# Attention outputs of three batches as plain float32 products, and decay arithmetic moved between VectorE, GpSimd and ScalarE

## The chip, the cores and the metric

The kernel runs on one core of a Trainium2 chip. The metric is the device time of one launch in microseconds (us). The engines are named as the profile names them: PE (TensorE's matmuls; PEld is its weight loads), DVE (VectorE), ACT (ScalarE), POOL (GpSimd) and SP (SyncE, which only issues DMAs here). Each engine takes its instructions in a fixed order, so whatever stands behind a waiting instruction waits too.

## The reference

Cut down, three parts that follow each other, for 4 batches of 768 tokens and 384 columns (8 heads of 48):

```python
def _attn_ref(q, k, v, a_re, a_im):
    mag = np.sqrt(a_re * a_re + a_im * a_im)
    scale = np.minimum(mag, 0.999) / (mag + 1e-06)
    a_re_n, a_im_n = (a_re * scale, a_im * scale)
    for t in range(S):
        new_re = ar * S_re - ai * S_im
        new_im = ar * S_im + ai * S_re
        S_re, S_im = (new_re + kv, new_im)
        y[:, :, t] = np.einsum('bhd,bhde->bhe', q[:, :, t], S_re)
def _moe_ref(x, U, V, w_ch1, w_ch2):
    u = x + (xt @ U @ V).transpose(0, 2, 1)
    return u + np.maximum(u @ w_ch1, 0.0) @ w_ch2
def _moe2_ref(x, w_ch1, w_ch2):
    u = x + np.real(fft2(x))
    return u + np.maximum(norm(u) @ w_ch1, 0.0) @ w_ch2
```

Here kv is the outer product of a token's key and value, xt is x transposed, and fft2 runs over tokens and columns. The first part is a linear attention with a complex decay for every token, head and channel; the other two are two-layer blocks with 1536 hidden columns.

## The kernel before, in words

The attention runs in chunks of 128 tokens, two chunks ("a pair") at a time: 6 chunks and 3 pairs to a batch, `m` counting the 12 pairs. Four generators of Python code build it.

- `decays(m)` works on tiles of 128 partitions by 768 columns (3 channel groups x 2 chunks x 128 tokens). L326 to L360 normalise the decays, take running products along the tokens (the scan of L340, one for each of 3 channel groups), and scale the queries (L359) and keys (L360). In batches 1 to 3 POOL does L325, L337, L349, L354 and L360, and L359 too in two pairs.
- `turns(m)` takes running sums of the angles (the scan of L381, three to a pair) and their sine and cosine, and L408 and L409 multiply queries and keys by these into the tile `QK`; POOL does one of the four products of each chunk. Six DMAs then move each chunk's `QK` into the transposed tile `QT`.
- `products(m, j)` works on one chunk: scores `sc` (L437), masked scores `pm` (L442), transposed keys `kp` (L451), outputs `y` and the contribution to the state `g` (both L469, in `summed`). Batch 0 and the first 4 chunks of batch 1 are `plain`: `y` and `g` are float32 products, head by head, of column halves of the array (0 to 63 and 64 up). From chunk 4 of batch 1 on, every factor is first split into two float16 parts (`ph`, `vh` and `vl`, `qh` and `ql`, `kh` and `kl`, `Sh` and `Sl`; POOL makes the low part of `ph` at L446 and of `Sl` at L568, ACT and DVE the others), and three float16 products, 128 columns wide, stand for one float32 product.
- `moe_units(0, ...)` is the first two-layer block. For each hidden step it multiplies into `hp` (9 matmuls, L91 to L93), ACT makes `hh` (L182) and DVE makes its low part `hl` (L184) with high priority, and one step later 9 matmuls add the step's output to `acc`.

`first_attention` runs batch 0's attention by itself. Then batch b's two-layer block runs with the attention of batch b + 1 spread between its steps (`Side`); batch 3's runs with the transform of batch 0 beside it; last come the second two-layer blocks. The order on every engine is fixed ahead by a scheduler that runs its own timing model over the priorities of this code (`schedule_with_timeline_sim`). Tiles named `t` come from a ring of 6 buffers, and a pair of batches 1 to 3 uses four of them (T, L, s, Th); slots tagged `x1` come from a ring of 3.

Of the kernel before, what the change touches and what calls it, by code (L numbers as in the profile page):

```python
# [8 lines left out]
F16 = mybir.dt.float16  # L9
# [12 lines left out]
DM = H * D  # L22
# [7 lines left out]
GSCALE = 2.0**-10  # L30
YSCALE = 2.0**-10 / FSCALE
# [10 lines left out]
def mixer_kernel(ctx, tc, a_in, qk_in, v_in, u_in, v4_in, w_in, cc_in, ss_in, cb_in, sb_in, id_in, mask_in, rows_in, out):  # L42
# [148 lines left out]
    # ------------------------------------------------------------------ attention  # L191
# [27 lines left out]
    def load(kind, m):  # L219
        """Decays, or queries and keys, of a pair of chunks."""  # L220
# [4 lines left out]
        if b == 0:  # L225
            t = wpl.tile(shape, F32, tag="w", name=name)
        else:
            t = attention_pool()(name, f"{kind}in", 1, shape)
# [3 lines left out]
    def load_vs():  # L232
        """All values of the first batch."""
# [15 lines left out]

    def row(x, i, js):  # L250
        return x[:, i, js].rearrange("p j t -> p (j t)")

    def parts(m):
        """The first pair goes chunk by chunk, so that its products start early."""
        return [slice(0, 1), slice(1, 2)] if m == 0 else [slice(0, 2)]

    def decays(m):
        """Decayed queries and keys of a pair of chunks and the tangents of its turns."""
# [3 lines left out]
        E = G if b else V  # L262

# [13 lines left out]
        ew[m] = T_, Th, qf, kf, ends  # L277
# [87 lines left out]
    def turns(m):  # L365
        """Rotates the queries and keys of a pair of chunks."""
        b, cc = PAIRS[m]
        at = attention_pool()
        T_, Th, qf, kf, ends = ew[m]
# [6 lines left out]
        for js in jj:  # L376
            cy = carry.get(b)
            t, th = T_[:, :, js], Th[:, :, js]
            n = 128 * (js.stop - js.start)
            for i in range(3):  # L380
                V.tensor_tensor_scan(  # L381
                    out=row(Th, i, js),
                    data0=one.to_broadcast([128, n]),
                    data1=row(T_, i, js),
                    initial=0.0 if cy is None else cy[:, i : i + 1],
                    op0=ALU.mult,
                    op1=ALU.add,
                )
# [12 lines left out]
            for j in range(js.start, js.stop):  # L401
# [14 lines left out]
    def products(m, j):  # L416
        """Scores, outputs and the next state of one chunk."""
# [4 lines left out]
        plain = b == 0 or b == 1 and c < 4  # L422
# [17 lines left out]
        def masked(hf):  # L440
            pm.append(room[:, hf] if b == 0 else at(f"pm{n}_{hf}", "pm", 2, (128, 4, 128)))
# [21 lines left out]
        def summed(out, rows, ops):  # L463
# [20 lines left out]
        if not plain:  # L484
# [3 lines left out]
            ph, plo = t3("ph", 1, (128, 2, 8, 128), F16).rearrange("p s h t -> s p h t")  # L488
# [9 lines left out]
        if not plain and c > 0:  # L498
# [726 lines left out]
```

## Time and profile before

| | |
|---|---|
| device time, 3 runs | 1037.37, 1039.2 and 1039.5 us; median 1039.2 |
| span of the profiled execution | 1035.1 us |
| what lies around the span | 2.3 to 4.4 us, by the three runs' times |
| busy, whole span | PE 885.1, DVE 690.3, POOL 443.3, ACT 441.3 us |
| 128 to 530 us (attention of batches 1 to 3 beside the first block) | PE 332.6, DVE 325.1, POOL 225.8, ACT 229.4 of 402 us; clock 0.90 |

The profiled execution has no time of its own beside its span; it is set against the three runs by what lies around it. A PE that is busy is not a PE at its peak, since matmuls overlap and their ends are modelled; PEclk is the granted clock as a share of the full 2.4 GHz.

### The profile page before, as it was taken

What the parts mean: (1) busy time and instruction counts of PE and PEld (TensorE: products, weight loads), DVE (VectorE), ACT (ScalarE), POOL (GpSimd) and SP (SyncE); (2) the same over time, 40 slices, a digit from 0 to 9 for tenths busy, and PEclk for the clock granted to TensorE, in tenths of its full rate; (3) what the DMA queues carried; (4) which work ended last, traced back from release to release, by engine and by line L of the source; (5) the groups of instructions that cost most, each with busy time, mean ns of one, the idle gap of its engine ahead of it and who ended that gap; (6) DMA issues with size and microseconds to landing.
All of it is one profiled execution on the core that took longest, in us unless ns stands there. A gap on an engine that the chain in (4) does not pass through costs nothing. (4 is left out here: it accounts for less than half of the span.)

```text
span 1035.1 us, 16471 instructions
## 1 busy us (share of the span) xinstructions
PE 885.1 (86%) x6338; PEld 841.7 (81%) x6338; DVE 690.3 (67%) x1104; ACT 441.3 (43%) x841; POOL 443.3 (43%) x426
## 2 busy tenths in 40 slices
PE   0059978788778787798899999779999999999997
PEld 0048777578777787787899999779999999999997
DVE  7997988897877689788764727886535554362121
ACT  6436565657545555555643224465212211222111
POOL 4445646575464645656446307776312222020000
PEclk9999899979898898989899999889999999999999
DMA  8078646834516152614135103342101021000000
GB/s 346 0 103 165 194 81 138 166 69 109 94 45 121 49 93 69 115 48 93 33 61 200 39 1 115 108 144 77 62 16 47 2 77 46 1 23 19 7 23 27
DMA packets 47097, 83.43 MB, mean 81 GB/s; under 512 B 5600, under 2 KB 36064, under 8 KB 47008
## 3 DMA queue, kind: packets, MB, share of 16 engines
q1 hardware_dynamic: 45152, 75.96, 30.8%
q0 software_dynamic: 1856, 6.31, 1.7%
q8 instruction: 52, 0.85, 0.4%
q14 instruction: 37, 0.30, 0.1%
HBM read 53.79 MB, written 9.44 MB: 61 GB/s over the span
## 5 line engine op out<-in xcount | busy, mean ns | idle before, releaser
L184 DVE SCALAR_TENSOR_TENSOR hl<-hp,hh 128x384 fp32r<-128x384 f32 x192 | 105.4, 551 | 191.8 <-ACT hh L182 186.6
L182 ACT ACTIVATE hh<-hp 128x384 fp32r<-128x384 f32 x192 | 93.1, 488 | 270.9 <-PE hp L93 249.1
L91 PE MATMUL acc<-w,hh 128*128 128x384 f32 x576 | 202.4, 352 | 2.0 <-ACT hh L182 2.0
L93 PE MATMUL acc<-w,hl 128*128 128x384 f32 x576 | 166.1, 352 | 38.4 <-DVE hl L184 38.2
L92 PE MATMUL acc<-w,hh 128*128 128x384 f32 x576 | 197.4, 343 | 0.0
L93 PEld LDWEIGHTS acc<-w,hl 128*128 128x128 f32 x576 | 106.9, 195 | 45.4 <-DVE hl L184 45.1
L91 PEld LDWEIGHTS acc<-w,hh 128*128 128x128 f32 x576 | 111.4, 193 | 4.3 <-ACT hh L182 3.0
L92 PEld LDWEIGHTS acc<-w,hh 128*128 128x128 f32 x576 | 111.5, 194 | 0.0
L91 PE MATMUL hp<-u,w 128*128 128x384 f32 x288 | 103.0, 359 | 6.2 <-ACT w L141 3.1
L92 PE MATMUL hp<-u,w 128*128 128x384 f32 x288 | 103.7, 360 | 1.2 <-POOL u L630 1.0
L93 PE MATMUL hp<-u,w 128*128 128x384 f32 x288 | 102.4, 356 | 0.0
L92 PE MATMUL hp<-n,w 128*128 128x384 f32 x288 | 96.9, 336 | 1.6 <-DVE n L920 1.6
L91 PE MATMUL hp<-n,w 128*128 128x384 f32 x288 | 96.5, 336 | 1.1 <-ACT n L919 1.1
L93 PE MATMUL hp<-n,w 128*128 128x384 f32 x288 | 96.8, 336 | 0.0
L437 PE MATMUL sc<-QT 96*128 96x128 f32 x384 | 66.6, 328 | 11.4 <-DMA QT<-QK 10.5
L437 PEld LDWEIGHTS sc<-QT 96*128 96x128 f32 x384 | 60.7, 232 | 14.3 <-issue 11.3
L142 POOL TENSOR_TENSOR w<-wxw,w 128x384 fp32r<-128x384 f32 x48 | 58.8, 1235 | 21.9 <-ACT w L141 21.7
L451 PE MATMUL kp<-ident,QK 128*128 128x128 f32 x120 | 20.5, 297 | 53.7 <-POOL QK L409 48.6
L91 PEld LDWEIGHTS hp<-u,w 128*128 128x128 f32 x288 | 58.5, 203 | 7.0 <-ACT w L141 3.3
L451 PEld LDWEIGHTS kp<-ident,QK 128*128 128x128 f32 x120 | 16.1, 155 | 55.5 <-POOL QK L409 48.6
L92 PEld LDWEIGHTS hp<-u,w 128*128 128x128 f32 x288 | 58.6, 203 | 2.2 <-POOL u L630 1.6
L93 PEld LDWEIGHTS hp<-u,w 128*128 128x128 f32 x288 | 58.3, 203 | 0.0
(302 smaller groups left out, 2056.4 us busy)
## 6 DMA issues: line engine op xcount, KB each, us to landing
QT<-QK SPq DMA_DIRECT2D x144, 129.0 KB
stw<-in_w_dram SPq DMA_DIRECT2D x48, 384.0 KB
ain<-in_a_dram SPq DMA_DIRECT2D x12, 768.0 KB
qkin<-in_qk_dram SPq DMA_DIRECT2D x12, 768.0 KB
x1d<-x SPq DMA_DIRECT2D x24, 192.0 KB
vin<-in_v_dram SPq DMA_DIRECT2D x18, 192.0 KB
lo<-x1d SPq DMA_DIRECT2D x12, 192.0 KB
out_dram<-lo SPq DMA_DIRECT2D x12, 192.0 KB
```

The lines of the kernel that those rows point to most:

```text
L91: T.matmul(o, ah, bh, start=start, stop=False, skip_group_check=skip)
L92: T.matmul(o, ah, bl, start=False, stop=False, skip_group_check=skip)
L93: T.matmul(o, al, bh, start=False, stop=stop, skip_group_check=skip)
L142: G.tensor_tensor(w[:, 1, zs], x, f32(w[:, 0, zs]), ALU.subtract)
L182: A.activation(hh, hp, AF.Relu)
L184: V.scalar_tensor_tensor(out=hl, in0=hp, scalar=0.0, in1=f32(hh), op0=ALU.max, op1=ALU.subtract)
L437: T.matmul(ps[:, h, :], q[:, 128:256], q[:, :128], start=True, stop=True)
L451: T.transpose(kp[z][:, i * 128 : (i + 1) * 128], QK[:, z, i, 128:256], ident)
```

## The change

Outputs `y` of batches 1 to 3 become float32 products of column halves in all chunks, as batch 0 has them; with them go `ph`, `qh`, `ql`, `Sh` and `Sl`. The state's `g`, on the other hand, becomes float16 products in the first 4 chunks of batch 1 as well. On the decays, L325 goes from POOL to ACT in batches 1 to 3 (9 pairs); L349 and L354 go from POOL to DVE there, L359 in 2 pairs; one scan takes the place of three, over 768 columns, with restarts from the constant tiles `starts` and `going`. The four products into `QK` become two, twice as wide, both on DVE. The angles are worked out in place in the tile of decays, of which there are now two by turns, so T and Th need no buffers; the count of L291 writes to an `x1` slot instead. The rest of the diff drops comments and moves constants.

```diff
+        s1, s2 = mk("L"), mk("s")
+        qf, kf = (qk[:, 0], qk[:, 1]) if b == 0 else (s1, s2)
+        Th, T_ = a[:, 0], a[:, 1]
...
-            E.tensor_scalar(s2_, s2_, -2e-6, 1.0, ALU.mult, ALU.add)
+            if b:
+                A.activation(s2_, s2_, AF.Identity, bias=one, scale=-2e-6)
+            else:
+                V.tensor_scalar(s2_, s2_, -2e-6, 1.0, ALU.mult, ALU.add)
...
-            n = 128 * (js.stop - js.start)
-            for i in range(3):
-                V.tensor_tensor_scan(out=row(s1, i, js), data0=starts[:, :n], data1=row(s1, i, js), initial=1.0, op0=ALU.max, op1=ALU.mult)
-        if b:
+            V.tensor_tensor_scan(out=flat(s1), data0=starts, data1=flat(s1), initial=1.0, op0=ALU.max, op1=ALU.mult)
+        if b and attp[1]:
             load("a", m + 1)
...
-            (G if m == 2 or b else V).tensor_tensor(th, s1_, th, ALU.mult)
+            (G if m == 2 else V).tensor_tensor(th, s1_, th, ALU.mult)
...
-            (G if m in (1, 2) or b else V).tensor_tensor(s1_, s1_, s2_, ALU.mult)
+            (G if m in (1, 2) else V).tensor_tensor(s1_, s1_, s2_, ALU.mult)
...
-            (G if m in (1, 2, 3, 4) else V).tensor_tensor(f, q, s1_, ALU.mult)
+            (G if m in (1, 2) else V).tensor_tensor(f, q, s1_, ALU.mult)
...
+            if len(jj) == 1:
+                if cy is not None:
+                    V.tensor_tensor(T_[:, :, 0, 0], T_[:, :, 0, 0], cy[:, :3], ALU.add)
+                V.tensor_tensor_scan(out=flat(Th), data0=going, data1=flat(T_), initial=0.0, op0=ALU.mult, op1=ALU.add)
+            else:
+                for i in range(3):
+                    V.tensor_tensor_scan(
...
-                for z, w in ((1, T_), (0, Th)):
-                    V.tensor_tensor(QK[:, z, :, :128], qf[:, :, j], w[:, :, j], ALU.mult)
-                    (V if z else G).tensor_tensor(QK[:, z, :, 128:256], kf[:, :, j], w[:, :, j], ALU.mult)
+                w = a[:, :, :, j]
+                V.tensor_tensor(QK[:, :, :, 128:256], kf[:, :, j].unsqueeze(1).to_broadcast([128, 2, 3, 128]), w, ALU.mult)
+                V.tensor_tensor(QK[:, :, :, :128], qf[:, :, j].unsqueeze(1).to_broadcast([128, 2, 3, 128]), w, ALU.mult)
+                for z in range(2):
...
-        plain = b == 0 or b == 1 and c < 4
+        plain = b == 0
...
+            pm.append(room[:, hf] if b == 0 else at(f"pm{n}_{hf}", "pm", 2, (128, 4, 128), pl=attp[1]))
             V.tensor_tensor(pm[hf], sc[hf], mask.unsqueeze(1).to_broadcast([128, 4, 128]), ALU.mult)
-            if not plain:
-                hs = slice(hf * 4, hf * 4 + 4)
-                A.copy(ph[:, hs], pm[hf])
-                G.tensor_tensor(plo[:, hs], pm[hf], ph[:, hs], ALU.subtract)
...
-                    for p in (slice(0, 64), slice(64, rows)) if plain else (slice(0, 128),):
+                    for p in (slice(0, 128),) if whole else (slice(0, 64), slice(64, rows)):
...
+        if not plain and not last:
             vh, vl = t3("vh", 2, (128, DM), F16), t3("vl", 2, (128, DM), F16)
             A.activation(vh, vin, AF.Copy, scale=VSCALE)
             V.scalar_tensor_tensor(out=vl, in0=vin, scalar=VSCALE, in1=vh, op0=ALU.mult, op1=ALU.subtract)
-            ph, plo = t3("ph", 1, (128, 2, 8, 128), F16).rearrange("p s h t -> s p h t")
...
-        if not plain and c > 0:
-            qh, ql = t3("qh", 1, (96, 8, 128), F16), t3("ql", 1, (96, 8, 128), F16)
-            A.copy(qh, QT[:, :, :128])
-            V.tensor_tensor(ql, QT[:, :, :128], qh, ALU.subtract)
...
-        if not plain and c > 0 and not isinstance(S, tuple):
-            S = t3("S", 2, (96, DM)), t3("Sh", 1, (96, DM), F16), t3("Sl", 1, (96, DM), F16)
-            A.activation(S[0], state[b], AF.Copy, scale=GSCALE * KSCALE * VSCALE)
-            A.copy(S[1], S[0])
-            G.tensor_tensor(S[2], S[0], S[1], ALU.subtract)
...
-        if plain:
-            ops = [(lambda h: pm[h // 4][:, h % 4], vin)]
-            if S is not None:
-                ops.append((lambda h: QT[:, h, :128], S))
-        else:
-            ops = [(lambda h: ph[:, h], vh), (lambda h: ph[:, h], vl), (lambda h: plo[:, h], vh)]
-            if S is not None:
-                pS, shi, slo = S
-                ops += [(lambda h: qh[:, h], shi), (lambda h: qh[:, h], slo), (lambda h: ql[:, h], shi)]
+        ops = [(lambda h: pm[h // 4][:, h % 4], vin)]
+        if S is not None:
+            ops.append((lambda h: QT[:, h, :128], S))
...
-                summed(gp, 128, [(hs(kh), vh), (hs(kh), vl), (hs(kl), vh)])
+                    G.tensor_tensor(sh, S.rearrange("p (h e) -> p h e", h=8), f3, ALU.mult)
+                summed(gp, 128, [(hs(kh), vh), (hs(kh), vl), (hs(kl), vh)], whole=True)
...
-            shi, slo = t3("Sh", 1, (96, DM), F16), t3("Sl", 1, (96, DM), F16)
-            A.copy(shi, sS)
-            G.tensor_tensor(slo, sS, shi, ALU.subtract)
-            state[b] = sS, shi, slo
+            state[b] = sS
```

The scheduler then orders every engine anew. Three places show what that does. On PE, in batch 2, chunk 1 (y_1 the output, g_1 the contribution to the state; the first number of a name is the chunk, the last only a buffer). Before:

```order
L469 LDWEIGHTS kh_1_2899
L469 MATMUL g_1_3015<-vh_1_2840,kh_1_2899 128x48
L469 LDWEIGHTS qh_1_2872
L469 MATMUL y_1_2947<-Sh_0_2809,qh_1_2872 128x48
L469 LDWEIGHTS kh_1_2899
L469 MATMUL g_1_3015<-vh_1_2840,kh_1_2899 128x48
L469 LDWEIGHTS qh_1_2872
L469 MATMUL y_1_2947<-Sh_0_2809,qh_1_2872 128x48
```

And now, at the same place on PE:

```order
L469 MATMUL y_1_2874<-vin_1_2669,pm_1_1_2828 64x48 x8
L469 MATMUL y_1_2874<-S_0_2718,QT_1_2298 64x48 x3
L469 LDWEIGHTS kh_1_2830
L469 MATMUL g_1_2926<-vh_1_2781,kh_1_2830 128x48
L469 MATMUL y_1_2874<-S_0_2718,QT_1_2298 64x48
L469 LDWEIGHTS kh_1_2830
L469 MATMUL g_1_2926<-vh_1_2781,kh_1_2830 128x48
L469 MATMUL y_1_2874<-S_0_2718,QT_1_2298 64x48
```

The two kinds of product alternate one by one in both, but now a column half of `y` stands between two full-width products of `g`; 94 halves of `y` in batches 2 and 3 stand so.

On DVE, in batch 2, the stretch around `hl` of hidden step 5 of the block of batch 1 (hl_1_0_5: batch, group, step; L, s and QK are the pair's tiles). Before:

```order
L184 SCALAR_TENSOR_TENSOR hl_1_0_4_2924<-hp_1_0_4_2885,hh_1_0_4_2922 128x384
L326 SCALAR_TENSOR_TENSOR L_4_3111<-L_4_3111,s_4_3112 128x768
L340 SCALAR_TENSOR_TENSOR L_4_3111<-starts,L_4_3111 128x256 x3
L461 SCALAR_TENSOR_TENSOR kl_2_3148<-kp_2_0_3151,kh_2_3147 128x8x48
L184 SCALAR_TENSOR_TENSOR hl_1_0_5_3046<-hp_1_0_5_3005,hh_1_0_5_3044 128x384
```

Now, on DVE:

```order
L412 TENSOR_TENSOR QK_3_2863<-L_2_2589,ain_2_2124 128x6x128
L183 SCALAR_TENSOR_TENSOR hl_1_0_4_2853<-hp_1_0_4_2818,hh_1_0_4_2851 128x384
L326 SCALAR_TENSOR_TENSOR L_4_3016<-L_4_3016,s_4_3017 128x768
L338 SCALAR_TENSOR_TENSOR L_4_3016<-starts,L_4_3016 128x768
L183 SCALAR_TENSOR_TENSOR hl_1_0_5_2957<-hp_1_0_5_2916,hh_1_0_5_2955 128x384
```

The normalisation and the running product still stand ahead of `hl`, the latter as one instruction.

On POOL, the instructions of the same pair around L325 and L337 (ph the float16 scores, T the tangents). Before:

```order
L568 TENSOR_TENSOR Sl_1_3050<-S_1_3016,Sh_1_3049 96x384
L325 TENSOR_SCALAR s_4_3112<-s_4_3112 128x768
L446 TENSOR_TENSOR ph_2_3105<-pm_2_0_3129,ph_2_3105 128x512
L337 TENSOR_TENSOR T_4_3110<-ain_4_2704,Th_4_3113 128x768
L446 TENSOR_TENSOR ph_2_3105<-pm_2_1_3143,ph_2_3105 128x512
```

Now, on POOL:

```order
L493 TENSOR_TENSOR QK_2_2840<-QK_2_2840 128x3x128
L337 TENSOR_TENSOR ain_4_2657<-ain_4_2657 128x768
L490 TENSOR_SCALAR fe_2_3012<-QT_2_2842 96x8
L493 TENSOR_TENSOR QK_2_2840<-QK_2_2840 128x3x128
```

Of the run of five, L337 is left, between two products with the chunk's end decays (L494 before, L493 now).

## Rows read from the trace of the kernel before

**Rows 1.** Busy time by stage, core 0; the header names the columns.
```profile
core 0: us, PE busy (x) PEld busy (x) DVE busy (x) ACT busy (x) POOL busy (x), PEclk, DMA share, GB/s
128.00:530.00 402.00, 332.61 (x2650) 310.37 (x2651) 325.08 (x428) 229.35 (x415) 225.79 (x195) 0.90 0.42 86
```

**Rows 2.** Waits of PE, 128 to 530 us: total us, times, longest us.
```profile
PE acc L93 <- DVE hl L184: 31.4, 12, 6.4
PE g L469 <- DVE kl L461: 15.1, 6, 5.4
```

**Rows 3.** Timeline of DVE: start us, length us, instruction, count, idle before.
```profile
341.99 4.79 DVE L326 SCALAR_TENSOR_TENSOR L<-L,s 128x768 f32<-128x768 f32 x1 [2.78 <-POOL s L325]
346.82 1.86 DVE L340 TENSOR_TENSOR_SCAN L<-starts,L 128x256 f32<-128x256 bf16 x3
```

**Rows 4.** Timeline of POOL, beside rows 3.
```profile
341.12 0.84 POOL L325 TENSOR_SCALAR s<-s 128x768 f32<-128x768 f32 x1
341.92 1.17 POOL L446 TENSOR_TENSOR ph<-pm,ph 128x512 f16<-128x512 f32 x1
343.05 1.81 POOL L337 TENSOR_TENSOR T<-ain,Th 128x768 f32<-128x768 f32 x1
344.82 1.15 POOL L446 TENSOR_TENSOR ph<-pm,ph 128x512 f16<-128x512 f32 x1
```

**Rows 5.** Timeline of PE around one stall.
```profile
160.42 0.91 PE L93 MATMUL acc<-w,hl 128*128 128x384 f32 x3 [2.63 <-DVE hl L184]
161.13 0.53 PE L91 MATMUL hp<-u,w 128*128 128x384 f32 x1
161.45 0.53 PE L92 MATMUL hp<-u,w 128*128 128x384 f32 x1
```

**Rows 6.** DVE's groups by shape, whole span: count, busy us, mean ns, idle before.
```profile
L340 DVE TENSOR_TENSOR_SCAN L<-starts,L 128x256 f32<-128x256 bf16 x36 | 37.6, 1097 | 0.1
L381 DVE TENSOR_TENSOR_SCAN Th<-one,cy,T 128x256 f32<-128x256 f32 x18 | 29.5, 1683 | 0.0
L326 DVE SCALAR_TENSOR_TENSOR L<-L,s 128x768 f32<-128x768 f32 x12 | 26.3, 2189 | 17.0 <-POOL s L325 16.8
L501 DVE TENSOR_TENSOR ql<-QT,qh 96x1024 f16<-96x1024 f32 x12 | 16.9, 1406 | 2.8 <-ACT qh L500 2.7
L354 DVE TENSOR_TENSOR L<-L,s 128x768 f32<-128x768 f32 x1 | 1.0, 959 | 0.0
```

**Rows 7.** Timeline of DVE: two scans while POOL rests.
```profile
18.18 1.26 DVE L340 TENSOR_TENSOR_SCAN L<-starts,L 128x256 f32<-128x256 bf16 x2
```

**Rows 8.** POOL's groups by shape, whole span, columns as in rows 6.
```profile
L446 POOL TENSOR_TENSOR ph<-pm,ph 128x512 f16<-128x512 f32 x28 | 36.6, 1309 | 26.4 <-ACT ph L445 26.4
L354 POOL TENSOR_TENSOR L<-L,s 128x768 f32<-128x768 f32 x11 | 25.1, 2285 | 14.5 <-DVE s L353 14.5
L409 POOL TENSOR_TENSOR QK<-s,Th 128x384 f32<-128x384 f32 x18 | 22.6, 1263 | 21.5 <-ACT Th L87 11.1 <-DVE pm L442 7.7 <-issue 2.7
L349 POOL TENSOR_TENSOR Th<-L,Th 128x768 f32<-128x768 f32 x9 | 16.5, 1828 | 27.3 <-ACT Th L348 27.3
```

**Rows 9.** Timeline of PE: float32 `y`, float16 `y`, float32 `g`, each with neighbours.
```profile
169.42 0.34 PE L92 MATMUL hp<-u,w 128*128 128x384 f32 x1
169.60 0.34 PE L93 MATMUL hp<-u,w 128*128 128x384 f32 x1
169.87 1.14 PE L469 MATMUL y<-vin,pm 128*64 128x48 f32 x32
170.94 0.44 PE L91 MATMUL acc<-w,hh 128*128 128x384 f32 x1
...
187.81 3.65 PE L469 MATMUL g<-vin,ke 128*64 128x48 f32 x32 [0.61 <-ACT ke L456]
...
252.53 0.31 PE L469 MATMUL y<-Sh,ql 96*128 96x48 f16 x6
252.68 0.42 PE L93 MATMUL hp<-u,w 128*128 128x384 f32 x1
```

More of the change, by code (lines that the diff above doesn't have):

```diff
@@ L29 @@
 VSCALE = 2.0**10
-GSCALE = 2.0**-10
-YSCALE = 2.0**-10 / FSCALE
+GSCALE = 1.0 / (KSCALE * VSCALE)
 RE_MID = 0.9
@@ L227, in load @@
         else:
-            t = attention_pool()(name, f"{kind}in", 1, shape)
+            later = kind == "a" and m % 2 == 0
+            t = attp[later].tile(shape, F32, tag=f"{kind}in", name=name, bufs=1)
         nc.sync.dma_start(t, {"a": a_in, "qk": qk_in}[kind][b, cs[0] // 2])
@@ L248, in mixer_kernel, with flat @@
     ew = {}
+    def flat(x):
+        return x.rearrange("p i j t -> p (i j t)")
     def row(x, i, js):
@@ L261, in decays @@
         a, qk = inp["a", m], inp["qk", m]
-        E = G if b else V
         def mk(nm):
             return at(f"{nm}{b}_{cc[0]}")
-        if b == 0:
-            T_, s1, s2 = a[:, 1], mk("L"), mk("s")
-            qf, kf = qk[:, 0], qk[:, 1]
-        else:
-            T_, s1, s2 = mk("T"), mk("L"), mk("s")
-            qf, kf = s1, s2
-        Th = a[:, 0] if b == 0 else mk("Th")
+        s1, s2 = mk("L"), mk("s")
+        qf, kf = (qk[:, 0], qk[:, 1]) if b == 0 else (s1, s2)
+        Th, T_ = a[:, 0], a[:, 1]
         use(LNEXP)
@@ L276, in decays @@
         jj = [slice(0, 2)]
-        ew[m] = T_, Th, qf, kf, ends
+        ew[m] = a, qf, kf, ends
         def of(js, *xs):
@@ L291, in steady @@
             V.scalar_tensor_tensor(
-                out=th if b else unread(js), in0=s2_, scalar=RE_LEAST, in1=re, op0=ALU.add, op1=ALU.is_le, accum_out=stat("re", b, cc[js.start])
+                out=unread(js), in0=s2_, scalar=RE_LEAST, in1=re, op0=ALU.add, op1=ALU.is_le, accum_out=stat("re", b, cc[js.start])
             )
@@ L368, in turns @@
         at = attention_pool()
-        T_, Th, qf, kf, ends = ew[m]
+        a, qf, kf, ends = ew[m]
+        Th, T_ = a[:, 0], a[:, 1]
         use(TRIG)
@@ L378, in turns @@
             t, th = T_[:, :, js], Th[:, :, js]
[L379 to L388, printed above, removed]
+            if len(jj) == 1:
[5 more added lines that the diff above has]
+                    V.tensor_tensor_scan(
+                        out=row(Th, i, js),
+                        data0=one.to_broadcast([128, 128]),
+                        data1=row(T_, i, js),
+                        initial=0.0 if cy is None else cy[:, i : i + 1],
+                        op0=ALU.mult,
+                        op1=ALU.add,
+                    )
             V.tensor_scalar(t, th, 1.0 / (2 * PI), MAGIC, ALU.mult, ALU.add)
@@ L461, in split, with summed @@
             V.scalar_tensor_tensor(out=dl, in0=src, scalar=KSCALE, in1=dh, op0=ALU.mult, op1=ALU.subtract)
-        def summed(out, rows, ops):
+        def summed(out, rows, ops, whole=False):
             for o, (l, r) in enumerate(ops):
@@ L483, in products @@
         scored.append(nc.cur_bb.bb.instructions[-1])
-        if not plain:
+        if not plain and not last:
             vh, vl = t3("vh", 2, (128, DM), F16), t3("vl", 2, (128, DM), F16)
@@ L508, in products @@
                 G.memset(kl[:, 768:], 0.0)
-            elif b == 0:
+            else:
                 ke = moe.tile([128, 8, 2, 48], F32, tag="u", name=f"ke{n}", bufs=5)
-            else:
-                ke = at(f"ke{n}", "ph", 1, (128, 1024), pl=attp[1])[:, :768].rearrange("p (h z x) -> p h z x", h=8, z=2)
             turned(0)
@@ L555, in products @@
                 if S is not None:
-                    G.tensor_tensor(sh, pS.rearrange("p (h e) -> p h e", h=8), f3, ALU.mult)
-                summed(gp, 128, [(hs(kh), vh), (hs(kh), vl), (hs(kl), vh)])
+                    G.tensor_tensor(sh, S.rearrange("p (h e) -> p h e", h=8), f3, ALU.mult)
+                summed(gp, 128, [(hs(kh), vh), (hs(kh), vl), (hs(kl), vh)], whole=True)
         x = xt[b, c] = xpl[0].tile([128, DM], F32, tag="x", name=f"x{n}", bufs=10)
-        A.activation(x, yp, AF.Copy, scale=1.0 / FSCALE if plain else YSCALE)
+        A.activation(x, yp, AF.Copy, scale=1.0 / FSCALE)
         yield
@@ L933, in mixer_kernel @@
     lnhalf = const("lnhalf", [128, 1])
-    starts = const("starts", [128, 2, 128], BF16)
     halfpi = const("halfpi", [128, 1])
@@ L941, in mixer_kernel @@
     G.memset(lnhalf, math.log(0.5))
-    G.memset(starts, 0.0)
-    G.memset(starts[:, :, 0:1], FSCALE**2)
-    starts = starts.rearrange("p x t -> p (x t)")
     G.memset(halfpi, PI / 2)
@@ L949, in mixer_kernel @@
     attp = [apool.enter_context(tc.tile_pool(name="att", bufs=2)), None]
+    starts = attp[0].tile([128, 6, 128], BF16, tag="starts", name="starts", bufs=1)
+    going = attp[0].tile([128, 3, 256], BF16, tag="going", name="going", bufs=1)
+    G.memset(starts, 0.0)
+    G.memset(starts[:, :, 0:1], FSCALE**2)
+    starts = starts.rearrange("p x t -> p (x t)")
+    G.memset(going, 1.0)
+    G.memset(going[:, :, 0:1], 0.0)
+    going = going.rearrange("p i t -> p (i t)")
     first = ExitStack()
@@ L966, in mixer_kernel @@
             with tc.issue_after(after):
-                T.matmul(warm, starts[:, :128], starts, start=True, stop=True, skip_group_check=True)
+                T.matmul(warm, starts[:, :128], starts[:, :256], start=True, stop=True, skip_group_check=True)
     first.close()
@@ L970, in mixer_kernel @@
     attp[1] = apool.enter_context(tc.tile_pool(name="halves", bufs=1))
+    load("a", 4)
     for b, g, f, half in moe_units(0, lambda b, g: uts[b, g], finish1, extra1):
```

2 lines of the change are left out of this document (removed).

## The prediction

> **What bounds the kernel now.** The stage table comes first. The attention of batches 1 to 3 runs from 128 to 530 us beside the first block's matmuls, and there PE is busy 332.6 of 402 us: it stands still for 69.4 us, and its granted clock is 0.90 [rows 1]. Only the two levels of 1.2 and 2.4 GHz occur, so 0.90 means the lower one for 20% of the stretch, about 80 us, and matmuls take about twice as long then: about 40 us more are lost. The reader is to see the second loss follow from the first. After a stall of 2.63 us the matmuls start 0.32 us apart (161.13, 161.45) [rows 5]; at full speed, with the same shape, they start 0.18 us apart (169.42, 169.60) [rows 9]. Stalls and slow clock together are worth 109 us, and this is the only stage where the change can gain much: after 530 us it touches nothing.
>
> The waits of PE come second. Of the 69.4 us, 31.4 end with DVE's `hl` and 15.1 with DVE's `kl` [rows 2]. Third comes what DVE did just before. The stall that ended at 349.18 us with `kl` is typical: DVE's L326 waited 2.78 us for POOL's L325, then took 4.79 us, and only behind it and the scan of L340 came `kl` [rows 3]. L326 has the size of L354, which takes 0.96 us undisturbed [rows 6]. During its 4.79 us POOL ran L446, L337 and L446 without a pause, from 341.92 to 345.97 us, and L326 ended 0.8 us later [rows 4]. So a DVE instruction that reads two tiles stands still while POOL works on tiles of its own. The groups say that this is no single case: two undisturbed scans of 256 columns take 1.26 us, 0.63 each [rows 7], while L340 has a mean of 1.10, L381 of 1.68 and L326 of 2.19 us [rows 6]. The excess of these three alone is 36 x 0.47 + 18 x 1.05 + 12 x 1.23 = 50 us of DVE time. PE is thus held up by DVE, and DVE by POOL.
>
> **The change, part by part.**
>
> POOL. L446 goes (36.6 us), nine of eleven L354 (9 x 2.285 = 20.6), the 18 products of L409 in batches 1 to 3 (22.6), the nine L349 (16.5) [rows 8], and the nine L325 (9 x 0.84 = 7.6) [rows 4]. That is 104 us; L568 and two of L359 go too, unpriced here. L494 comes eight times more, at most 8 x 1.15 by the like of L446 [rows 4], so 9 us. Of 225.8 us in the stage [rows 1], somewhat under half goes, about half with the unpriced ones. What stays are mainly L337 and L360 of each pair.
>
> DVE, at undisturbed prices. It gains nine `th` and nine `s1` products at 0.96 (L349, L354), 17.3 us, two of L359 at 0.96, 1.9 us, and the fourth `QK` product of 18 chunks, half the size, which I estimate at half of 0.96, 8.6 us. `kl` comes eight times more, also half-size, 3.8 us. Eight additions of 3 columns cost between nothing and a short scan (0.63); I take 0.25, 2 us. `ql` goes, 16.9 us [rows 6]. A scan of 768 columns lies between 0.63 us (length free) and 1.89 (three of 256); I take 1.89, nearest in columns, so merging gains nothing by itself. Sum: +17 us of work. Against it stands the excess of 50 us; if half of it goes with half of POOL's work, DVE ends at about 325 + 17 - 25 = 317 us, hardly less busy. What changes is how long `hl` and `kl` stand behind something: three scans gave POOL three chances to come between, one gives one, and of the three POOL instructions during L326 one remains in the new order.
>
> The stalls. I take the share that goes to be POOL's share, half: 35 us of standing still, and with it half of the slow clock, 20 us. Bounds: none, if L337 and L360 fill the same gaps, and nine tenths, if only their length remains.
>
> PE's own work. A `y` of float16 parts is 48 products for a chunk with a state, 24 for one without; they start 0.15 / 6 = 0.025 us apart (252.53 to 252.68) [rows 9], so 1.2 and 0.6 us. A float32 `y` is two sets, or one, at 1.07 us (169.87 to 170.94), so 2.14 and 1.07. Fourteen chunks change, twelve with a state: 12 x 0.94 + 2 x 0.47 = +12.2 us. `g` of four chunks in batch 1 falls from 3.65 to 24 x 0.025 = 0.6 us: -12.2 us. These cancel.
>
> They don't cancel where the new order puts one column half of `y` between two full-width products of `g`, 94 times. Two halves side by side now cost 0.067 us each (1.07 / 16); `g`, whose halves differ in width, costs 3.65 / 16 = 0.228 us each [rows 9]. If a lone half costs what a half of `g` does, that is 0.16 us more. Passing from full width to halves adds 0.27 - 0.18 = 0.09 us (169.42, 169.60, 169.87) [rows 9], twice per half of `y`, 0.18 us. Bounds are 0 and 0.34 us; the row of `g` may already hold part of the passing, so I take 0.26: 94 x 0.26 = +24 us, at most 32.
>
> The Trainium skill has a rule here that speaks against the change: "TensorEngine Tiling (Array Packing)", section Key Properties, says that a change of the tiling mode, not only of the tile, drains TensorE. The 0.09 us on entering the halves agrees with it; no row here shows the modes alternating with each product. By the rule the sum takes the upper 32 us and comes out at 1016 us; were a change free, it would be 984 us.
>
> ACT takes L325's nine instructions, at most 0.96 us each by the like of L354, but loses the casts of `ph`, `qh` and `Sh`; it is busy 229 of 402 us [rows 1], so its idle time hides them. If that cover fails, `hh` behind them is up to 0.96 us late.
>
> Added waits. `pm` is now read by PE itself from two buffers, so the next chunk's masking on DVE waits for this chunk's `y`, with `hl` queued behind it. The scores of the next chunk come after that `y` in the code as well, so I take 0; a wait of one set (1.07 us) at each of 15 boundaries within batches would be 16 us. L291 now needs a slot of a ring of 3 and can wait for its last reader; what queues behind is L313, and then `hl`. The ring gives back the T and Th buffers in return; 0. Two tiles of decays let the next load start a pair earlier; it ends no stall above, so 0.
>
> Before 128 us, scans merge too and a POOL product per chunk comes to DVE, and all six DMAs of a chunk now wait for both wide products. By half-size prices that is 0.48 us a chunk against at most 2 x 0.63 a pair saved: 0, within 5 us either way.
>
> Sum: -35 - 20 + 24 = -31 us on a span of 1035.1, so 1004 us; the median of the runs lies 4.1 us above the span, so 1008 us.
>
> **Rivals.** *Nearly every stall goes.* For it: in rows 3 and 4 two of three instructions that held L326, and the wait before it, disappear. Against: DVE stays as busy, and a static order leaves gaps. At nine tenths: -62 - 36 + 24 = -74, so 965 us. 20%.
>
> *Slower: halves of `y` between full-width `g`.* The place is PE in batches 2 and 3, the price 0.34 us x 94 = 32 us, more at the lower clock; stalls return only a tenth (-11), since L337 and L360 remain, and DVE's 17 us more delay PE in today's ratio of 69 to 325, +4. Sum +25, 1064 us. It decides when stalls and clock return less than 32 of 109 us, three tenths. For it: the order and the 0.09 us; against: much of the alternation ran at 0.025 us a product before. 15%.
>
> *No gain.* The stalls fall by a fifth (-22) because what POOL keeps still comes just ahead of `hl`, and the alternation takes it back (+24): 1041 us, about where it was. For it: `hl` keeps its place behind L326 and the scan in the new DVE order. 10%.
>
> **How the numbers follow.** The forecast, 1008 us, gets 55%, with its own range of 985 to 1030, from the shares of a third to two thirds of the stalls. The range of 968 to 1045 us takes in most of the first rival and the third, and leaves out 1 in 10 above and 1 in 10 below. A measurement can tell about 0.2% from no change. Faster: 55% + 20% + 2% of the third rival, 77%; within 0.2%: 6%; slower: 15% + 2%, 17%.
>
> **What would show it.** Right: POOL at 110 to 130 us in the attention stage; L326 and the scans near their undisturbed lengths; PE's waits for `hl` and `kl` at half of 46.5 us; the clock at 0.95. The price of alternation is the distance between starts of `y` and `g` where they take turns: 0.09 us a pair if free, 0.35 if I am right. Wrong: waits for `hl` as long as before with POOL half empty (then DVE's own work holds it), or PE held by `pm`, or a span before 128 us that moves by more than 5 us.

## The result and the profile after

The changed kernel takes 1049.0 us (median of 4 runs, 1046.89 to 1051.72), the kernel before 1038.86 us beside it: a ratio of 1.0098, 95% interval 1.0075 to 1.0121. It is slower by 1%, where 1008 us and a gain of 3% were forecast. The profiled execution has a span of 1046.6 us against 1035.1.

The stage of [rows 1], 128 to 530 us, in the changed kernel (same columns):

```profile
128.00:530.00 402.00, 351.36 (x2839) 328.52 (x2840) 268.73 (x405) 217.81 (x391) 127.17 (x138) 0.88 0.47 90
```

POOL fell from 225.8 to 127.2 us and DVE from 325.1 to 268.7, PE stands still for 50.6 us instead of 69.4, and yet the granted clock went down, from 0.90 to 0.88. Most of what DVE lost is stretching, and `ql` is gone (16.9 us); its groups by shape over the whole span, which answer to [rows 6]:

```profile
L338 DVE TENSOR_TENSOR_SCAN L<-starts,L 128x768 f32<-128x768 bf16 x12 | 27.8, 2315 | 0.2
L381 DVE TENSOR_TENSOR_SCAN ain<-going,ain 128x768 f32<-128x768 bf16 x11 | 19.2, 1749 | 0.2 <-ACT ain L86 0.2
L326 DVE SCALAR_TENSOR_TENSOR L<-L,s 128x768 f32<-128x768 f32 x12 | 14.5, 1211 | 3.6 <-ACT s L323 3.4
```

L326 went from 2.19 to 1.21 us, and the scan of L381 stands at 1.75 us, one length for all of them. The scan of L338, beside which POOL still runs L337, has a mean of 2.32 us. The waits of PE in the same stretch answer to [rows 2] (total us, times, longest us):

```profile
PE sc L441 <- DMA QT<-QK: 16.5, 2, 16.2
PE acc L90 <- ACT hh L181: 11.9, 4, 4.5
PE sc L441 <- DMA stw<-in_w_dram: 6.0, 1, 6.0
PE acc L92 <- DVE hl L183: 4.5, 3, 2.3
```

`hl` is down from 31.4 to 4.5 us and `kl` from 15.1 to 0.8. Other waits stand in their place: the scores wait 16.2 us for `QT` once and 6.0 us just behind the weight loads, and `hh` is up from 1.6 to 11.9 us.

To see where the time went, both traces are cut at the same pieces of work: the start of the first block (its first `hp` matmul), its 109th, 541st and 577th `hp` matmul of 864, the last of them, and the end. Before, and under it the changed kernel (columns as in rows 1, the second number is the length):

```profile
0.00:133.00 133.00, 68.11 (x687) 55.07 (x687) 115.97 (x165) 69.85 (x127) 68.57 (x59) 0.97 0.61 157
133.00:218.40 85.40, 71.78 (x540) 63.17 (x541) 74.29 (x100) 55.06 (x99) 51.41 (x39) 0.90 0.57 117
218.40:524.40 306.00, 253.76 (x2017) 241.37 (x2017) 241.71 (x314) 170.27 (x307) 168.20 (x151) 0.89 0.39 80
524.40:547.70 23.30, 22.60 (x265) 21.95 (x265) 16.80 (x28) 11.66 (x25) 11.40 (x12) 1.00 0.36 61
547.70:675.60 127.90, 121.20 (x752) 118.26 (x751) 79.40 (x147) 43.85 (x94) 66.87 (x74) 0.97 0.30 98
675.60:1035.10 359.50, 347.60 (x2085) 341.88 (x2083) 162.12 (x355) 90.65 (x191) 76.89 (x94) 0.99 0.12 40
```

```profile
0.00:133.20 133.20, 64.14 (x687) 51.33 (x687) 114.81 (x153) 71.18 (x130) 59.09 (x51) 0.91 0.60 157
133.20:232.30 99.10, 65.63 (x528) 60.80 (x528) 67.83 (x105) 57.48 (x101) 41.19 (x40) 0.82 0.54 108
232.30:511.50 279.20, 263.36 (x2156) 248.90 (x2157) 188.49 (x282) 151.66 (x271) 79.72 (x87) 0.91 0.45 84
511.50:554.80 43.30, 43.30 (x310) 37.72 (x309) 13.49 (x22) 7.30 (x17) 4.16 (x7) 0.76 0.19 38
554.80:686.20 131.40, 123.08 (x755) 119.61 (x755) 80.28 (x150) 43.72 (x93) 66.97 (x74) 0.96 0.30 95
686.20:1046.60 360.40, 348.74 (x2084) 343.34 (x2083) 160.32 (x351) 90.47 (x190) 75.20 (x92) 0.98 0.12 39
```

The middle of the stage gains as forecast: 306.0 us became 279.2. Two other stretches give it back and more. From 133 to 232 us the work takes 13.7 us longer, with PE standing still for 33.5 us instead of 13.6. From 511 to 555 us it takes 20.0 us longer, with PE never idle and a clock of 0.76.

The first stretch. The count of L288 for pair 4 is the first row here, on DVE; behind it come L326 of that pair, and on PE the scores that wait for what follows:

```profile
133.40 0.95 DVE L310 SCALAR_TENSOR_TENSOR L<-s,L 128x768 f32<-128x768 f32 x1
...
176.85 0.94 DVE L288 SCALAR_TENSOR_TENSOR un<-s,ain 128x768 bf16<-128x768 f32 x1
...
182.81 0.95 DVE L326 SCALAR_TENSOR_TENSOR L<-L,s 128x768 f32<-128x768 f32 x1
```

```profile
203.82 0.34 PE L635 MATMUL acc<-zst,vst 128*128 128x384 f32 x1
220.35 0.98 PE L441 MATMUL sc<-QT 96*128 96x128 f32 x3 [16.20 <-DMA QT<-QK]
```

L310, which stands behind L288 in the code, ran at 133.40 us: the pair's squares were there. L288 reads the tile `s`, which a logarithm overwrites next, so the rest of the pair waits for it. L288 needs an `x1` slot, and in DVE's fixed order it comes 43 us later, behind 8 `hl` of the first block. In the kernel before (L291) it stood behind 3, ran at 147.40 us, and L326 at 153.99. The second stretch is a run of turns between halves of `y` and full-width products of `g`, here on PE:

```profile
517.91 0.20 PE L469 MATMUL g<-vh,kh 128*128 128x48 f16 x1
518.04 0.32 PE L469 MATMUL y<-S,QT 96*64 96x48 f32 x2
518.29 0.20 PE L469 MATMUL g<-vh,kh 128*128 128x48 f16 x1
...
519.41 0.20 PE L469 MATMUL g<-vl,kh 128*128 128x48 f16 x1
519.54 0.45 PE L469 MATMUL y<-S,QT 96*64 96x48 f32 x2
519.93 0.22 PE L469 MATMUL g<-vl,kh 128*128 128x48 f16 x1
520.08 0.45 PE L469 MATMUL y<-S,QT 96*64 96x48 f32 x2
```

A float32 product is two records in the trace, so `x2` is one half of `y`. One turn (a `g` and one half of `y`) takes 0.38 us (517.91 to 518.29), and from 519.4 us on 0.52. The windows say why: PE is busy throughout, and the clock falls to its lower level in the middle of the turns.

```profile
515.00:522.00 7.00, 7.00 (x89) 5.61 (x83) 2.74 (x4) 0.88 (x2) 1.05 (x3) 0.82 0.33 112
519.50:526.30 6.80, 6.80 (x39) 6.25 (x40) 1.25 (x2) 1.42 (x4) 1.07 (x3) 0.50 0.64 127
```

Six of the 14 falls of the clock in the block are of this kind: in the 6 us before them PE is never idle and takes such turns. The other five:

```profile
328.30:331.70 3.40, 3.40 (x23) 3.17 (x23) 1.04 (x2) 2.25 (x5) 0.25 (x2) 0.50 0.38 153
382.90:389.70 6.80, 6.80 (x40) 6.32 (x40) 2.66 (x4) 3.87 (x9) 3.11 (x4) 0.50 0.57 86
464.90:471.70 6.80, 6.80 (x35) 6.43 (x35) 3.02 (x5) 5.05 (x9) 0.25 (x2) 0.50 0.21 86
492.20:499.00 6.80, 6.80 (x39) 6.05 (x38) 3.94 (x7) 3.21 (x6) 1.87 (x4) 0.50 0.00 1
536.50:550.20 13.70, 13.70 (x72) 11.08 (x73) 1.25 (x2) 1.11 (x3) 0.00 (x0) 0.50 0.01 2
```

Together the six keep the clock down for 44.3 us, half of which, 22 us, is lost. The kernel before shows the like behind the `g` of [rows 9], whose float32 halves differ in width (64 and 32 columns): PE is busy, and the clock falls at 191.6 us.

```profile
187.80:191.60 3.80, 3.79 (x34) 2.82 (x34) 3.80 (x6) 1.19 (x3) 2.79 (x3) 1.00 0.86 136
191.60:195.00 3.40, 3.34 (x11) 2.80 (x10) 2.53 (x6) 2.58 (x4) 1.84 (x3) 0.51 1.06 196
```

### The profile page after: what moved, and what is told of

Its sections match the earlier page's. It is cut to its first block, busy times and chain, and to the rows that moved or that the text cites. A ratio compares the mean times of both kernels' runs of the same rounds, so it can differ in the third digit from the quotient of the medians.

```text
span 1046.6 us, 16609 instructions
## 1 busy us (share of the span) xinstructions
PE 908.2 (87%) x6514; PEld 861.7 (82%) x6514; DVE 625.2 (60%) x1058; ACT 421.8 (40%) x799; POOL 326.3 (31%) x351
## 3 DMA queue, kind: packets, MB, share of 16 engines
q1 hardware_dynamic: 45152, 75.96, 31.4%
## 4 chain that ended last, share of the span: by engine, by line
PE 60%; DVE 19%; DMA 10%; issue 4%; ACT 3%; SPq 2%; POOL 1%; DVEq 0%; ACTq 0%; POOLq 0%
PE acc L90 7%; PE hp L91 7%; PE hp L92 7%; PE acc L92 7%; PE hp L90 7%; PE acc L91 7%; PE y L469 4%; DMA stw<-in_w_dram 4%; DMA ain<-in_a_dram 3%; PE sc L441 3%; DMA QT<-QK 3%; PE g L469 3%; DVE L L338 2%; DVE wxw L124 2%; SPq L416 2%
## 5 line engine op out<-in xcount | busy, mean ns | idle before, releaser
L90 PE MATMUL acc<-w,hh 128*128 128x384 f32 x576 | 202.7, 352 | 13.8 <-ACT hh L181 13.7
L441 PE MATMUL sc<-QT 96*128 96x128 f32 x384 | 64.1, 324 | 27.4 <-DMA QT<-QK 19.0
L441 PEld LDWEIGHTS sc<-QT 96*128 96x128 f32 x384 | 58.9, 231 | 29.5 <-issue 21.5
L451 PE MATMUL kp<-ident,QK 128*128 128x128 f32 x120 | 22.6, 317 | 57.3 <-DVE QK L411 57.3
L141 POOL TENSOR_TENSOR w<-wxw,w 128x384 fp32r<-128x384 f32 x48 | 52.9, 1112 | 29.3 <-ACT w L140 28.1
L90 PEld LDWEIGHTS hp<-u,w 128*128 128x128 f32 x288 | 58.4, 204 | 3.1 <-ACT u L608 2.9
L91 PEld LDWEIGHTS hp<-u,w 128*128 128x128 f32 x288 | 58.6, 203 | 2.6 <-POOL u L609 1.3
L86 ACT ACTIVATE ain<-ain 128x768 f32<-128x768 f32 (+1 forms) x50 | 40.5, 812 | 47.2 <-DVE ain L393 47.1
```

Of the source, the lines that this page charges most:

```text
L86: ordered(lambda: A.activation(*args, **kw))
L90: T.matmul(o, ah, bh, start=start, stop=False, skip_group_check=skip)
L91: T.matmul(o, ah, bl, start=False, stop=False, skip_group_check=skip)
L141: G.tensor_tensor(w[:, 1, zs], x, f32(w[:, 0, zs]), ALU.subtract)
L441: T.matmul(ps[:, h, :], q[:, 128:256], q[:, :128], start=True, stop=True)
L451: T.transpose(kp[z][:, i * 128 : (i + 1) * 128], QK[:, z, i, 128:256], ident)
```

## The experiments

Two theories came from this. **Ring:** L288 waits for an `x1` slot behind the weight loads of the first block, which use the same three slots, and so pair 4 is late. **Turns:** each change between halves and full width costs time of PE, and it costs the clock as well. Their rivals are named in the expectations.

All kernels are compared by one split of the first block, from its first `hp` matmul to its last. Idle is its length less PE's busy time in the windows. Clock is half of the time that PE was busy at the lower level, by the record of the granted clock. Work is what is left. For before: 542.6 = 73.3 + 39.0 + 430.4. For the changed kernel: 553.0 = 57.6 + 45.8 + 449.6. All in us; start is what lies before the block, rest what lies behind; changes counts where `y` and `g` follow each other in the trace. The split in a row is of one execution, the profiled one; the median is of all runs. The profiled execution of e11, at 1028.1 us, is the fastest of its ten, and e2's has the highest granted clock of its ten (0.958; the lowest is 0.933), so a difference of a few us in one column says little.

| kernel | median | ratio to before (95%) | changes | start | idle | clock | work | rest |
|---|---|---|---|---|---|---|---|---|
| before | 1038.9 | | 356, equal width | 133.0 | 73.3 | 39.0 | 430.4 | 359.5 |
| changed | 1049.0 | 1.0075 to 1.0121 | 200 | 133.2 | 57.6 | 45.8 | 449.6 | 360.4 |
| e1 own tile | 1066.3 | 1.0214 to 1.0278 | 263 | 141.3 | 44.4 | 51.4 | 459.8 | 368.1 |
| e2 y whole | 1034.1 | 0.9929 to 0.9975 | 41, equal width | 138.3 | 58.5 | 24.9 | 449.4 | 361.1 |
| e3 g after y | 1017.3 | 0.9752 to 0.9807 | 15 | 135.2 | 63.7 | 23.8 | 429.6 | 361.3 |
| e4 before, ring | 1059.0 | 1.0146 to 1.0204 | 180, equal width | 132.8 | 90.7 | 39.9 | 433.4 | 361.3 |
| e5 e3 + own tile | 1000.4 | 0.9611 to 0.9713 | 18 | 133.8 | 52.7 | 16.8 | 432.0 | 361.5 |
| e6 e3 + POOL back | 1046.8 | 1.0060 to 1.0120 | 13 | 136.8 | 75.2 | 36.6 | 427.0 | 366.4 |
| e7 before, g after y | 1049.0 | 1.0081 to 1.0126 | 20 | 132.6 | 80.3 | 38.9 | 433.7 | 360.2 |
| e8 products mixed | 1042.3 | 1.0021 to 1.0062 | 187 | 133.2 | 48.9 | 44.0 | 450.6 | 362.4 |
| e9 products ordered | 1037.4 | 0.9967 to 1.0004 | 15 | 133.6 | 68.4 | 35.1 | 431.4 | 366.6 |
| e11 g in halves | 1035.9 | 0.9957 to 0.9994 | 111, equal width | 133.8 | 65.3 | 26.5 | 440.9 | 359.9 |
| e12 e5 + k on DVE | 999.8 | 0.9602 to 0.9660 | 16 | 131.3 | 46.5 | 31.0 | 429.3 | 362.5 |
| e13 own tile, turns kept | 1046.0 | 1.0036 to 1.0078 | 249 | 132.6 | 45.0 | 43.4 | 458.2 | 364.7 |

**e3, the order of g.**

```diff
         summed(yp, 128, ops)
+        ylast = nc.cur_bb.bb.instructions[-1]
...
-                summed(gp, 128, [(hs(kh), vh), (hs(kh), vl), (hs(kl), vh)], whole=True)
+                with tc.issue_after(ylast):
+                    summed(gp, 128, [(hs(kh), vh), (hs(kh), vl), (hs(kl), vh)], whole=True)
```

> The changed kernel, but the products of g are issued only behind the last product of y of their chunk, with y still in halves. Alternation theory: about 100 turns lose 0.2 us each and part of the slow clock goes, 1026 us (1018 to 1036), no better than whole-width y. Rival theory, float32 halves are dear by themselves wherever they stand: 1049 us, within 4.

It took 1017.3 us, 32 us less than the changed kernel and 0.7 below the range. Work fell by 20.0 us, back to that of the kernel before, and the clock's loss by 22.0; idle rose by 6.1. Each of the nine falls of the clock in e3's block follows idle time of PE; those within turns are gone. No run of the changed kernel had a granted clock above 0.934, none of e3 below 0.949. The late stretch, 43.3 us before this edit, took 26.7 at full clock:

```profile
499.00:525.70 26.70, 25.34 (x314) 24.22 (x313) 13.00 (x24) 7.28 (x17) 4.69 (x8) 1.00 0.38 68
```

The turns are the larger part of the loss, and half of their price is the clock.

**e2, y at full width.** The edit: `summed(yp, 128, ops, whole=b > 0)`.

> The changed kernel, but the float32 products of y in batches 1 to 3 are of all 128 columns (8 in a set) instead of two halves of 64 (16 in a set). Alternation theory: y and g no longer change between halves and full width; the about 100 turns of two halves and one g that took 0.375 us (0.16 us if they stood apart) lose 0.2 us each, and the slow clock that comes in such stretches at 519 and 536 us goes with it: 20 us of work and some 5 to 10 of clock, 1022 us (1015 to 1032). Rival theory, float32 is dear in itself in any shape: 1049 us, within 4.

1034.1 us, a miss by 2 us, and 17 more than e3, where e3 was expected to be no better. The clock's loss fell by 20.9 us, twice what was expected, but work not at all. The 264 products of `y` took 60.8 us of PE, 0.23 us each, where e3 has 528 halves in 34.1 us, 0.13 us for two. Full width removes the changes and costs as much itself.

**e11, g in halves.** The edit: `whole=True` is left out for `g`.

> The changed kernel, but g of batches 1 to 3 is in two column halves of 64, as y is, still of float16 parts; y and g take turns as before (about 180 changes between them). If the change of width is what costs, y and g at equal width start about 0.07 us apart where they take turns, and the slow clock of such stretches goes: about 100 turns x 0.2 us and 20 us of clock come back, less 360 more products of g at up to 0.067 us, 24 us: 1030 us (1020 to 1042). If the change between float32 and float16 costs, the turns cost as much as before or more, with twice as many products of g: 1060 us or above.

1035.9 us, in the range. PE takes turns between float32 halves of `y` and float16 halves of `g` here:

```profile
515.93 0.30 PE L469 MATMUL y<-S,QT 96*64 96x48 f32 x4
516.07 0.20 PE L469 MATMUL g<-vh,kh 128*64 128x48 f16 x2
516.10 0.30 PE L469 MATMUL y<-S,QT 96*64 96x48 f32 x4
516.23 0.20 PE L469 MATMUL g<-vh,kh 128*64 128x48 f16 x2
```

Two halves of `y` (four records) and two of `g` take 0.17 us. At the full clock the first `y` starts 0.024 us behind a `g` and a `g` 0.052 us behind a `y` (medians); in the changed kernel it is 0.126 and 0.154 us. So a change of width costs 0.10 us, and changing the data type at one width next to nothing. That is 0.20 us a turn, which on about 100 turns is the 20 us of work.

**e7, the same order in the kernel before.** As e3, in the kernel before.

> The kernel before, but g of the float16 chunks is issued only behind the last product of y of its chunk. There y and g are both of full width and take turns without a change of width. If the change of width is what costs, nothing is gained: 1040 us, within 5. If taking turns costs by itself (another PSUM bank with each product), the 350 turns are worth what they are in the changed kernel, 0.15 us each, and 1000 to 1010 us come out.

It gained nothing, and lost more than expected, 11 us (1038.0 us for before in this comparison). Work did not fall (433.7 against 430.4): the 356 changes at equal width were free. In the kernel before, `y` and `g` start 0.025 us behind each other at the full clock, as the products within each do (medians). Of the loss 7 us are idle, 80.3 against 73.3; what made them was not followed up.

**e4, the ring in the kernel before.**

```diff
-                out=th if b else unread(js), in0=s2_, scalar=RE_LEAST, in1=re, op0=ALU.add, op1=ALU.is_le, accum_out=stat("re", b, cc[js.start])
+                out=unread(js), in0=s2_, scalar=RE_LEAST, in1=re, op0=ALU.add, op1=ALU.is_le, accum_out=stat("re", b, cc[js.start])
```

> The kernel before with one edit: the unread result of L291 in batches 1 to 3 goes to a slot of the x1 ring instead of Th. Ring theory: L291 of pair 4 (147.4 us before) goes behind the weight loads to about 175 us, scores of that pair are late, and the kernel before loses about the 14 us that the changed one lost at the same place: 1053 us (1046 to 1060). Rival theory, the load and the QT copies: 1039 us, within 3.

18.7 us slower than before (1040.33 us in this comparison), by one operand. L291 of pair 4 moved from 147.40 to 169.94 us, behind 8 `hl` instead of 3, and PE shows the same wait for the same scores:

```profile
216.08 3.76 PE L437 MATMUL sc<-QT 96*128 96x128 f32 x16 [15.44 <-DMA QT<-QK]
```

**e1, e13 and e5, an own tile.**

```diff
+            if b:        # e1; "if m > 3:" in e5 and e13
+                return flat(mk("un"))[:, :384].bitcast(BF16).rearrange("p (i j t) -> p i j t", i=3, t=128)
             return slot(f"un{m}").bitcast(BF16)[:, :n].rearrange("p (i j t) -> p i j t", i=3, t=128)
```

> The changed kernel, but for batches 1 to 3 the unread result of L288 goes to a tile of its own instead of a slot of the x1 ring of three that the weight loads share. Ring theory: L288 of pair 4 (176.85 us in the changed kernel) moves to about 150 us, the wait of 16.2 us for scores at 220 us goes, and the 14 us that the stretch 133 to 232 us lost against before come back: 1035 us (1028 to 1040). Rival theory, the late load of that pair's decays (124 us against 93) and QT copies that wait for both wide products: the load is where it was, so 1049 us, within 3.

A miss: 1066.3 us. The wait went (L290 of pair 4 ran at 137.03 us, and idle fell by 13.2), but the new order has 263 changes, work rose by 10.2 us, the clock's loss by 5.6, and 8 us each were lost before and behind the block.

> The changed kernel with the own tile of e1 from pair 4 on only, so that pair 3 keeps its slot as in e5; y and g take turns 247 times (changed kernel 198, e1 261). Theory that the loss of e1 is the start, which its pair 3 delays by 8 us, and more turns, not the tile: the start is back at 133 us, the wait of 16 us for scores is gone (-13), 49 turns more cost 49 x 0.1 = 5 us of work and some clock, and what e1 lost after the first block (8 us) is open: 1049 - 13 + 5 to 10 = 1044 us (1038 to 1055). Rival, the own tile costs 17 us by itself: 1066 us, within 4.

1046.0 us: the start is back, and idle is 12.6 us lower than in the changed kernel. Work rose by 8.6 us, of which the 49 changes more are 5 at 0.10 us each, and the rest by 4.3. So the tile does not cost 17 us by itself, but with the turns left in it gives only 3 us. That the turns take all the remainder is not shown.

> As e3 (g behind y), and the unread result of L288 goes to a tile of its own from pair 4 on. With the alternation gone, the ring theory is tested again: the 16.2 us wait for scores near 220 us goes, and of the 1017 us of e3 some 10 come back, as in the stretch 141 to 230 us of e1 (88.7 us against 99.1): 1007 us (1000 to 1013). If what the stall gives back there is only lost again further on, 1017 us, within 3. Rival, an own tile costs by itself, as the 17 us of e1 could suggest: 1030 us or more.

1000.4 us, 17 less than e3 (15 if each is set against the kernel before of its own comparison; one of the four runs took 1009.7 us): idle fell by 11.0 and the clock's loss by 7.0. L290 of pair 4 ran at 132.61 us, and the stretch that had become 99.1 us took 84.7:

```profile
133.80:218.50 84.70, 65.17 (x521) 59.26 (x522) 68.67 (x100) 57.29 (x103) 40.55 (x42) 0.88 0.58 120
```

It beats the kernel before by 2.9 to 3.9%.

**e6, POOL's work back.** In e3, four lines are given back to POOL, such as

```diff
-            (G if m == 2 else V).tensor_tensor(th, s1_, th, ALU.mult)
+            (G if m == 2 or b else V).tensor_tensor(th, s1_, th, ALU.mult)
```

> As e3 (g behind y), but in batches 1 to 3 four wide operations of each pair are on GpSimd again, where the kernel before had them: the scaling of s (L323), the products of L347 and L352, and in pairs 3 and 4 that of L357. POOL gets about 9 x (0.84 + 1.83 + 2.29) = 45 us more work, DVE about 17 us less. Theory that POOL's work holds up DVE and DVE holds up PE: L326 and the scan are stretched again, PE's waits for hl and kl come back to 30 us or more, and the time is 1017 + 20 to 35 = 1045 us (1035 to 1055). Rival, DVE's own length decides: DVE has less to do, and the time is 1017 us or somewhat less (1008 to 1020).

1046.8 us, 29.5 more than e3, as expected; not by the waits I named. Between 133 and 560 us `hl` was waited for 2.5 us and `kl` 15.0 us, but `hh` 15.1 and `QT` 18.2. Idle rose by 11.5 us, the clock's loss by 12.8. DVE gave away 20 wide products, 19 us at 0.95, and was as busy in the block as in e3 (349.88 and 350.08 us), because the rest was stretched; L326 was not (1.13 against 1.38 us). DVE also waited 11.5 us for the products of L347 and 4.3 for the scaling of `s`, which POOL now makes, so what the stretching costs and what the slower products cost is not told apart. The scan of L381 (L378 here), which takes 1.75 us in e3:

```profile
L378 DVE TENSOR_TENSOR_SCAN ain<-going,ain 128x768 f32<-128x768 bf16 x9 | 22.3, 2476 | 0.9 <-ACT ain L86 0.7
```

**e9 and e8, the products alone.** The kernel before with `products` of the changed one; in e9 with `g` behind `y`, in e8 without.

> The kernel before with the part of the change in the products alone, and g behind y: y of batches 1 to 3 as float32 halves, all g of these batches of float16 parts, no parts of pm, q and S. The decays, turns, scans and the unread result stay as before, with their work on GpSimd. POOL loses L446 (36.6 us) and keeps the rest. If the products and their order are worth most of what e3 gains: 1040 less 10 for y and g (66.3 us before, 49.8 in e3) less some 5 to 10 of stalls: 1022 us (1014 to 1030). If the gain of e3 comes from the moved element-wise work alone: 1040 us, within 4.

> As e9 (the kernel before with the products of the change alone), but without the order of g behind y, so that they take turns again (187 changes). By the alternation theory it is as much slower than e9 as the changed kernel is than e3, 32 us: 1069 us (1060 to 1075). If the 32 us there came from another thing that the order of g moves, 1037 us, within 5.

e9, expected at 1022, is level with before at 1037.4, so the products alone give none of the gain of e5. e8 was expected at 1069 and took 1042.3, just outside the rival's range. The turns did cost 19.2 us of work and 8.9 of clock against e9, but idle fell by 19.5, of which 9.8 are waits for `hl` and `kl`: with POOL's work where it was, PE would have stood still in much of that time anyway.

**e12, one more product on DVE.** In e5, L358 goes to DVE.

> As e5, but the product of k and s2 (L358) of batches 1 to 3 is on VectorE too, so that of the wide products only L337 is left on GpSimd. POOL loses 9 x 2.5 = 22 us more, DVE gains 9 x 0.96 = 9 us. Theory that POOL's work holds up DVE: what DVE loses to it (L326, L338 and what else runs beside L358's 3.2 us) is more than 9 us, and 1000 falls to 994 us (988 to 1000). Rival, DVE's own length now decides: 1005 us or more.

999.8 us, just inside the range but level with e5's 1000.4, so it shows neither. In the profiled execution idle fell by 6.2 us more and the clock's loss rose by 14.2; over all four runs the mean granted clock is 0.957 against 0.960 in e5. Why the clock was lower is open.

## Why the prediction was wrong

In the sum the prediction had -35 for stalls, -20 for the clock and +24 for PE's turns. Measured against before, in the changed kernel: idle -15.6, clock +6.7, work +19.2, start and rest +1.1, together 11.4 of the 11.5 us of span. The error of 41 us is 27 on the clock, 19 on the stalls, less 5 on the turns.

- **POOL: right. DVE: more relief than forecast.** POOL is at 127 us (110 to 130 forecast) and L326 near its undisturbed length. The waits for `hl` and `kl` fell from 46.5 to 5.3 us, where half was forecast, and e6 shows that the place of four of POOL's operations decides 29 us. But DVE is at 269 us, not at 317. In the block the scans and L326 lost 46 us, where 25 were taken, and the `QK` products take 9 us less, not 9 more. The 768-column scan was taken at 1.89 us and takes 1.75 undisturbed. The wait for `pm`, taken as 0, is 1.2 us.
- **The turns' work: right.** 94 places x 0.26 = 24 us against 20, and 0.38 us for a turn against 0.35 forecast. That `y` and `g` otherwise cancel holds too: work is 430.4 us before and 429.6 in e3. The rule of the Trainium skill, "TensorEngine Tiling (Array Packing)", section Key Properties, that a change of the tiling mode drains TensorE, agrees: 0.126 and 0.154 us where the width changes, 0.024 and 0.052 in e11, where it doesn't.
- **The clock: the first step that failed.** It was tied to the stalls alone: half of the stalls, so half of the slow clock, -20 us. Instead it rose by 6.7. The clock also falls inside a run of turns, with PE busy all the time: six such falls lose 22 us, and e3 gets 22.0 us back by the order of `g`. Once the turns are gone and the ring is relieved (e5), the clock's loss is 22.2 us below that of before. That this meets the 20 us is luck, since idle has fallen by 28% there, not by half. Nor do the two go together elsewhere: e3 has 63.7 us of idle with 23.8 of clock, e12 46.5 with 31.0. The prediction had the falls within turns only as "more at the lower clock" in the rival, though one fall of the kind stood in the trace of before, right behind its [rows 9].
- **The slot of L291: the second.** "The ring gives back the T and Th buffers in return; 0." It costs 15 to 17 us (e3 to e5) or 19 (before to e4); with the turns left in, taking it back gives only 3 (e13). The buffers that came back were not the ones that L288 now needs; while the first block's weights still load, each of the three `x1` slots turns over at the pace of those loads. The order could have told it: on DVE this count of pair 4 stands behind 3 `hl` in the kernel before, behind 8 in the changed kernel and in e4, and behind none in e5. I looked at the order in batch 2, where no weights load.
- **The size of the stalls: too large by itself too.** Even in e5, without both faults, idle falls by 20.6 us, not 35. In the block the waits for `hl` and `kl` fall from 53.4 to 18.9 us there, but those for `hh` and `QT` rise from 1.6 to 16.5. The sum let no other wait take the place of those that go.

Of the rivals, the one on the slow side (1064 us) had the place and its condition: stalls and clock together return 8.9 us, less than 32. Its 32 us for the turns were meant as work, of which 20 came; the 31.7 us of e3 hold the clock as well. What held the stalls and the clock back was not L337 and L360, as it said, but the clock under the turns and the ring. Taken off one after the other, the turns (31.7) and then the slot (16.9) lead from 1049.0 to 1000.4 us, where the prediction had 984 without the turns' price. This is no check that the two add up: with the turns left in, the slot gives 3 us.

Open: e7's 11 us, what lengthens the rest by 4 to 9 us in e1, e6, e9 and e13, and whether the products of the kernel before would do as well with the rest of the change, which was not tried.

## What to carry to other kernels

When a result that nobody reads is moved to another buffer, list who else takes slots of that ring, and in which stage: the price of the slot here was the wait for the weight loads (18.7 us in e4), not the store. When products of different tile widths meet on TensorE, look at the order that comes out, count the changes, and keep each width together; one ordering constraint was worth 32 us here. Where the widths were equal (e7), the same constraint cost 11. And a cost on an engine is only paid where that engine does not wait anyway: the same 19 us of turns cost 5 us in e8 and 32 in the changed kernel.

## What the hardware showed

- A change between column halves and full width costs 0.10 us on PE each way (float32 halves and float16 full width, e11). Taking turns at one width is free, with one data type (before, e7) or two (e11).
- The granted clock fell to 1.2 GHz within runs of such turns six times, once in a stretch in which the profile has PE busy 7.00 of 7.00 us. A busy share does not say that the clock is safe.
- For float32 products of 48 columns, two halves cost 0.13 us (e3) and one full-width product 0.23 us (e2).
